# Attention scores by 64-key tiles in a fused attention and feed-forward kernel: eight tiles in the array, ten score steps per query block

## The chip, the cores and the metric

The kernel runs on one core of one Trainium2 chip. The metric is device time in microseconds (us), from the launch to the end on that core. A profile of one execution gives the span from the first to the last instruction, which is a little shorter than that time.

The core's engines appear under short names. PE is the matrix unit, TensorE; PEld is its loading of weights. DVE is VectorE, ACT is ScalarE, POOL is GpSimd, SP is the queue that issues most transfers. Matrix results land in PSUM, a small memory of eight banks that TensorE writes and VectorE and ScalarE read. Everything else lies in SBUF.

## The reference, cut to what matters

One layer norm feeds two branches, and both are added to the input.

```python
S, D = 2048, 448
def _A_ref(x, wqkv, wo):
    H = 16; Dh = D // H; W = 256            # 16 heads of 28
    q, k, v = ...                           # of x @ wqkv
    scores = jnp.einsum("bhqd,bhkd->bhqk", q, k) * (Dh ** -0.5)
    idx = jnp.arange(S)
    mask = (idx[:, None] - idx[None, :] >= 0) & (idx[:, None] - idx[None, :] < W)
    scores = jnp.where(mask[None, None], scores, -1e9)
    p = _softmax(scores, axis=-1)
    o = jnp.einsum("bhqk,bhkd->bhqd", p, v)
    return o.transpose(...).reshape(B, S, D) @ wo
def _B_ref(x, w_gate, w_up, w_down):        # F = 1792
    return (_gelu(x @ w_gate) * (x @ w_up)) @ w_down
xn = _layernorm(x, axis=-1)
return x + _A_ref(xn, A_wqkv, A_wo) + _B_ref(xn, B_w_gate, B_w_up, B_w_down)
```

A query sees only itself and the 255 keys before it. So 128 keys are seen by at most 383 queries, and 64 keys by at most 319.

## The kernel before

The 2048 tokens are worked through in four blocks of 512 queries (`qb` 0 to 3). The 16 heads are four groups `g` of four heads; each head has 32 of the 128 partitions (28 and padding). A block has two stretches. In the attention stretch, scores, exponentials and values of the four groups are interleaved with dense matrix work from "feeds": the output and down projection of the block before (`po`), the projections of the next block (`pv`, `pq`, `pk`), and some up projections ahead of time (`ue`). In the gated stretch the rest of gate (`gt`) and up (`u`) follows.

One group takes three score steps, so a block takes twelve. Each step fills the same PSUM tile of four banks, 512 columns for each of the four heads, from two key tiles of 128 keys:

```python
def pieces(qb, n):             # (key tile, first query, queries, column), and which columns are masked
    k = 4 * qb
    if n == 0:
        return [(k + 3, 384, 128, 0), (k, 0, 384, 128)], [(0, 2, True), (384, 1, False)]
    if n == 1:                 # (cut: block 0)
        return [(k + 1, 128, 384, 0), (k - 2, 0, 128, 384)], [(0, 1, True), (256, 2, False)]
    return [(k - 1, 0, 256, 0), (k + 2, 256, 256, 256)], [(128, 1, False), (256, 1, True)]

# attention(), one step: scores, exponential, masks        (score tile "s": one buffer)
for kt, q0, nq, col in pc:
    for j in range(4):
        r = slice(32 * j, 32 * j + 32)
        nc.tensor.matmul(ss[:, j, col:col + nq], lhsT=kT[r, g, kt * P:(kt + 1) * P],
                         rhs=qT[r, g, qb * QB + q0:qb * QB + q0 + nq], start=True, stop=True,
                         tile_position=(32 * j, 0), skip_group_check=True)
p_sb = work.tile([P, 4, QB], bf16, name="p_sb", bufs=4)
nc.scalar.activation(out=p_sb[:, :, 0:ncol], in_=ss[:, :, 0:ncol], func=ACT.Exp, scale=SCALE)
for col, nb, diag in runs:     # ... 128 or 256 columns of each head, on all partitions
    nc.gpsimd.affine_select(out=reg, in_=reg, pattern=mid + [[1 if diag else -1, P]], ...)
```

Four matmuls, each on 32 rows of the array, share it. The values of a group come one group later, at step 4, 7 or 10, and for the last group in the gated stretch. Four matmuls on 32 columns each share the array, and all 128 keys of a tile are contracted at once:

```python
def pv(g, steps):
    tag = "o" if qb == 0 else "m" if g < 3 else down_tag[0]
    ov = psum.tile([P, QB], f32, name="ov", tag=tag, bufs=2 if tag == "m" else 1)
    # ... for each piece and j in 0..3
    nc.tensor.matmul(ov[32 * j:32 * j + 32, q0:q0 + nq], lhsT=v_sb[:, kt, h, :], rhs=p_sb[:, j, col:col + nq],
                     start=..., stop=..., tile_position=(0, 32 * j), skip_group_check=True)
    oc = work.tile([P, QB], f32, name="oc", bufs=2)
    nc.vector.tensor_copy(out=oc[:, :], in_=ov[:, :])
```

A column of ones in `v_sb` gives the sum of the weights as one more row of `ov`. `inverse()` brings it out by two 32x32 transposes and a reciprocal on VectorE (`l1`, `l_all`, `ri`, `rb`), and `scale_o()` multiplies, on GpSimd:

```python
nc.gpsimd.tensor_tensor(out=oN[:, g, :], in0=oc[:, :], in1=rb[...], op=ALU.mult)
```

In blocks 1 and 2 the feeds carry one pair of up projections, in block 3 five, in block 0 two; each goes from PSUM to SBUF by two casts (`hT<-ue`), and the gate's result is multiplied onto it later (`hT<-ge,hT`). The other pairs take the gate times `u` from PSUM (`hT<-ge,u`). The feeds of blocks 1 to 3 use the two PSUM banks tagged "m".

Of the kernel before, what the change touches and what calls it, by code (L numbers as in the profile page):

```python
# [68 lines left out]
def drain(feeds):  # L69

    while any(f.gens for f in feeds):
        min((f for f in feeds if f.gens), key=lambda f: (f.held, f.closed)).run()
# [3 lines left out]
def kernel(  # L76
# [63 lines left out]

    eps_t = const.tile([P, 1], f32, name="eps_t")
    nc.vector.memset(eps_t[:, :], 1e-5)
    warm = const.tile([P, 512], bf16, name="warm")
    nc.vector.memset(warm[:, :], 0.0)
    wqp = const.tile([P, 3, H, 32], bf16, name="wqp")
    wkp = const.tile([P, 3, H, 32], bf16, name="wkp")
    w3p = const.tile([P, H, 32], bf16, name="w3p")
    nc.vector.memset(wqp[:, :, :, Dh:32], 0.0)
    nc.vector.memset(wkp[:, :, :, Dh:32], 0.0)
    nc.vector.memset(w3p[:, :, Dh:32], 0.0)  # L150
    nc.vector.memset(wo[:, :, :], 0.0)
    nc.scalar.preload_act_table_set("natural_log_exp_and_others")

    xnT = const.tile([P, 4, S], bf16, name="xnT")
# [6 lines left out]
    def warmup(n):  # L161
        wps = phase[0].pool.tile([P, 4, QB], f32, name="wps", tag="s")
        for i in range(n):
            nc.tensor.matmul(wps[:, i % 4, :], lhsT=warm[:, 0:P], rhs=warm[:, :], start=True, stop=True)


    def stat(t):
# [126 lines left out]
    def new_hT(qb):  # L294
        hT = blk.tile([P, NF, QB], bf16, name="hT", tag="hT")
        hTs[qb] = hT
# [81 lines left out]
                dense(b, False)  # L378
                end(b)

    def pieces(qb, n):

        k = 4 * qb
        if n == 0:
            return [(k + 3, 384, 128, 0), (k, 0, 384, 128)], [(0, 2, True), (384, 1, False)]
        if n == 1:
            if qb == 0:
                return [(k + 1, 128, 384, 0)], [(0, 1, True), (256, 1, False)]
            return [(k + 1, 128, 384, 0), (k - 2, 0, 128, 384)], [(0, 1, True), (256, 2, False)]
        if qb == 0:  # L390
            return [(k + 2, 256, 256, 0)], [(0, 1, True)]
        return [(k - 1, 0, 256, 0), (k + 2, 256, 256, 256)], [(128, 1, False), (256, 1, True)]

    def attention(qb, feeds, aux, plan):
        oN = blk.tile([P, 4, QB], bf16, name="oN")
        oNs[qb] = oN
        pend, copied, later = [], [], []

        def inverse():
            while copied:  # L400
                g, oc = copied.pop(0)
                l1 = work.tile([P, 16, 32], f32, name="l1", bufs=1)
                nc.vector.transpose(out=l1[:, :, :].rearrange("p a b -> p (a b)"), in_=oc[:, :])
                nc.vector.tensor_copy(out=l_all[:, 4 * qb + g, :], in_=l1[:, :, Dh])
                ri = work.tile([P, 16], f32, name="ri")
                nc.vector.reciprocal(out=ri[:, :], in_=l_all[:, 4 * qb + g, :])
                rb = work.tile([P, 16, 32], f32, name="rb", bufs=2)
                nc.vector.transpose(out=rb[:, :, :], in_=ri[:, :].unsqueeze(2).to_broadcast([P, 16, 32]))  # L408
                later.append((g, oc, rb))

        def scale_o():
            while later:
                g, oc, rb = later.pop(0)
                nc.gpsimd.tensor_tensor(out=oN[:, g, :], in0=oc[:, :], in1=rb[:, :, :].rearrange("p a b -> p (a b)"), op=ALU.mult)  # L414

        def pv(g, steps):

            tag = "o" if qb == 0 else "m" if g < 3 else down_tag[0]
            ov = psum.tile([P, QB], f32, name="ov", tag=tag, bufs=2 if tag == "m" else 1)
            for n, pc, p_sb in steps:  # L420
                for i, (kt, q0, nq, col) in enumerate(pc):
                    for j in range(4):
                        h = 4 * g + j
                        nc.tensor.matmul(ov[32 * j:32 * j + 32, q0:q0 + nq], lhsT=v_sb[:, kt, h, :], rhs=p_sb[:, j, col:col + nq],  # L424
                                         start=(n == 0 and i == 0), stop=(n == 2 and i == len(pc) - 1), tile_position=(0, 32 * j),
                                         skip_group_check=True)
            oc = work.tile([P, QB], f32, name="oc", bufs=2)
            nc.vector.tensor_copy(out=oc[:, :], in_=ov[:, :])  # L428
            copied.append((g, oc))

        if qb:
            feeds[0].run()
        for g in range(4):
            while (qb, g) not in done:
                feeds[0].run()
            group = []
            for n in range(3):
                pc, runs = pieces(qb, n)
                ncol = sum(x[2] for x in pc)
                for fd in feeds:  # L440
                    if fd.held:
                        fd.run()
                inverse()
                if n == 1 and g:
                    pv(g - 1, pend.pop(0))
                ss = phase[0].pool.tile([P, 4, QB], f32, name="sc", tag="s")
                for kt, q0, nq, col in pc:
                    for j in range(4):
                        r = slice(32 * j, 32 * j + 32)
                        nc.tensor.matmul(ss[:, j, col:col + nq], lhsT=kT[r, g, kt * P:(kt + 1) * P],  # L450
                                         rhs=qT[r, g, qb * QB + q0:qb * QB + q0 + nq], start=True, stop=True,
                                         tile_position=(32 * j, 0), skip_group_check=True)
                p_sb = work.tile([P, 4, QB], bf16, name="p_sb", bufs=4)
                nc.scalar.activation(out=p_sb[:, :, 0:ncol], in_=ss[:, :, 0:ncol], func=ACT.Exp, scale=SCALE)  # L454
                for col, nb, diag in runs:
                    reg = p_sb[:, :, col:col + nb * P]
                    if nb > 1:
                        reg = reg.rearrange("p h (b q) -> p h b q", q=P)
                    mid = [[0, 4], [0, nb]] if nb > 1 else [[0, 4]]
                    nc.gpsimd.affine_select(out=reg, in_=reg, pattern=mid + [[1 if diag else -1, P]], compare_op=ALU.is_ge,  # L460
                                            fill=0.0, base=0 if diag else -1, channel_multiplier=-1 if diag else 1)
                group.append((n, pc, p_sb))
                scale_o()
                left = 12 - 3 * g - n
                if left == 1:
                    drain(feeds)
                elif not qb:
                    share(feeds + [Feed()], 1e12, 0)
                else:
                    to = plan.get(12 - left, 0)  # L470
                    i = 12 - left
                    whole = sum(f.left for f in feeds) + STEP * left + PV * sum(j > i for j in (4, 7, 10))
                    ahead = STEP + (PV if n == 0 and g else 0) + (360 if to > 1000 else 0)
                    late = 400 if i == 0 else 0
                    share(feeds, (whole - late) / (left + 0.2) + late - ahead - to, to)
                if aux:
                    aux.pop(0)()
            pend.append(group)

        def rest():  # L480
            pv(3, pend.pop(0))
        def after():
            inverse()
            scale_o()
        return rest, after


# [63 lines left out]
    for qb in range(NB):  # L551
# [4 lines left out]
        if qb == 0:  # L556
            new_hT(0)
            early = (2, 8)
            feeds = [Feed((v23, 360), (gen_qk(0, (1, 2, 3)), 3 * QK1), (gen_proj(1), PROJ), (gen_up(0, early), UP1 * len(early)))]
            feeds[0].held = True  # L560
        else:
            ring[0] = ("m",)
            tags = "dodo" if last_tag[0] == "o" else "odod"
            feeds = [Feed((gen_down(qb - 1, tags), DOWN))]
            if qb < 3:
                feeds.append(Feed((gen_proj(qb + 1), PROJ)))
                new_hT(qb)
                early = (2,)
                feeds[1].gens.append(gen_up(qb, early))
                feeds[1].left += UP1  # L570
                plan = {0: 1140, 2: 1140, 4: 1300, 5: 1300, 7: 1300, 8: 1300, 10: 1300}
            else:
                new_hT(3)
                early = (2, 4, 6, 8, 10)
                feeds.append(Feed((gen_up(3, early), UP1 * len(early))))
                plan = {1: 1300, 4: 1300, 5: 1300, 7: 1300, 10: 1300}
        if qb:
            score_pool(1)
        rest, after = attention(qb, feeds, aux, plan)
# [19 lines left out]


    g1 = work.tile([P, 512], f32, name="g1", tag="l1", bufs=1)
    g2 = work.tile([P, 512], f32, name="g2", tag="rb", bufs=2)
    okc = const.tile([P, 1], f32, name="okc")
    okb = const.tile([P, 1], bf16, name="okb")
    one = const.tile([P, 1], bf16, name="one")
# [131 lines left out]
```

## Time and profile before

| | |
|---|---|
| time, median of 3 | 233.24 us (232.87 to 233.63) |
| span of the profiled execution | 230.8 us |
| mean granted TensorE clock | 0.997 |
| exponential `p_sb<-sc`, four heads of 512 columns | 40 times, mean 1877 ns |
| selects `p_sb<-p_sb`, 128x512 | 64 times, mean 634 ns |
| selects `p_sb<-p_sb`, 128x1024 | 28 times, mean 1098 ns |
| `oc<-ov` on VectorE | 16 times, mean 690 ns |
| `oN<-oc,rb` on GpSimd | 16 times, mean 1358 ns |
| score matmuls, value matmuls | 352 each |

How to read it. An engine's busy time is the time in which it had an instruction under way. Matmuls are pipelined, and each has a latency that the next one does not wait for; so a matmul's duration is longer than its cost, and the cost of a burst is read from its start to the start of what follows. A form such as `32*128 32x384` is a matmul on 32 rows and 128 columns of the array, with a moving operand of 32 partitions and 384 columns. In an answer of the timeline the columns are start, duration, engine, line, operation, tiles, form and count; in square brackets stands the engine's idle time before it and what ended it.

### The profile page before, as it was taken

To read this page: it belongs to the slowest core of one execution; us is meant where nothing else is said; L and a number is where in the kernel's file an instruction comes from. 1 tells how busy PE (TensorE), PEld (TensorE's weight loads), DVE (VectorE), ACT (ScalarE), POOL (GpSimd) and SP (SyncE) were. 2 spreads that over 40 slices of the span, in tenths; PEclk is the share of its full clock that TensorE was granted. 3 is DMA by queue.
4 is the path that set the end of the run, shared out by engine and by line. 5 is a ranking of instruction groups with operands and counts; after the bars stand their busy time and mean duration, and the time that the engine had idled before them with its cause. 6 is when DMAs were issued, how large, how long until landed. Compare 5 with 4: busy or idle time off the path is not lost.

```text
span 230.8 us, 4154 instructions
## 1 busy us (share of the span) xinstructions
PE 221.0 (96%) x1686; PEld 94.0 (41%) x1686; DVE 136.8 (59%) x280; ACT 135.1 (59%) x115; POOL 93.9 (41%) x116
## 2 busy tenths in 40 slices
PE   7889999999999999999999999999999999999990
PEld 2433333344443444344444444344444344334470
DVE  6996877869536676655534686464432866486210
ACT  3678897425967766333767767233687777363000
POOL 5024767220257877020066776320055877320000
PEclk9999999999999999999999999999999999999998
DMA  6917999012100000012100000000000000000010
GB/s 219 315 27 82 330 328 306 13 23 50 23 20 3 21 23 17 5 23 45 24 23 0 22 1 20 23 0 0 3 0 20 23 0 23 20 0 0 26 54 19
DMA packets 15682, 12.52 MB, mean 54 GB/s; under 512 B 7400, under 2 KB 14632, under 8 KB 15656
## 3 DMA queue, kind: packets, MB, share of 16 engines
q1 hardware_dynamic: 15112, 11.38, 17.7%
q10 hardware_dynamic: 544, 0.80, 1.0%
q8 instruction: 15, 0.25, 0.5%
q14 instruction: 11, 0.09, 0.1%
HBM read 8.77 MB, written 1.84 MB: 46 GB/s over the span
## 4 chain that ended last, share of the span: by engine, by line
PE 84%; ACT 5%; DVE 4%; DMA 2%; issue 1%; SPq 0%; ACTq 0%
PE po L285 18%; PE gt L202 16%; PE u L202 11%; PE sc L450 6%; PE gt L207 5%; PE po L280 5%; PE ov L424 4%; ACT p_sb L454 4%; PE pq L202 4%; PE ue L202 4%; PE pk L202 4%; PE pv L202 3%; DMA wv<-in_A_wqkv_dram 2%; PE pq L207 2%; PE ue L207 1%; DVE st L169 1%
## 5 line engine op out<-in xcount | busy, mean ns | idle before, releaser
L460 POOL TENSOR_SCALAR_AFFINE_SELECT p_sb<-p_sb 128x512 bf16<-128x512 bf16 (+1 forms) x92 | 69.4, 775 | 87.8 <-ACT p_sb L454 87.5
L454 ACT ACTIVATE p_sb<-sc 128x2048 bf16<-128x2048 f32 (+2 forms) x48 | 85.0, 1771 | 23.8 <-PE sc L450 22.2
L360 ACT ACTIVATE ge<-gt 128x1024 bf16<-128x1024 f32 x28 | 28.7, 1023 | 43.5 <-PE u L207 18.6
L285 PE MATMUL po<-wd,hT 128*128 128x448 bf16 (+1 forms) x238 | 50.1, 342 | 0.0
L202 PE MATMUL gt<-xnT,wg 128*128 128x512 bf16 x168 | 40.5, 380 | 0.0
L364 DVE TENSOR_TENSOR hT<-ge,u 128x512 bf16<-128x512 bf16 x38 | 24.4, 682 | 16.8 <-ACT ge L360 16.7
L414 POOL TENSOR_TENSOR oN<-oc,rb 128x512 bf16<-128x512 f32 x16 | 21.7, 1358 | 23.2 <-DVE rb L408 23.2
L285 PEld LDWEIGHTS <-hT 128*128 128x128 bf16 x238 | 21.6, 98 | 20.0 <-issue 4.0
L202 PE MATMUL u<-xnT,wu 128*128 128x512 bf16 x114 | 27.7, 379 | 0.0
L202 PEld LDWEIGHTS <-wg 128*128 128x128 bf16 x168 | 15.1, 98 | 22.1 <-issue 6.0
L202 PEld LDWEIGHTS <-wu 128*128 128x128 bf16 x168 | 15.7, 98 | 19.4 <-issue 1.8
L428 DVE COPY oc<-ov 128x512 f32<-128x512 f32 x16 | 11.0, 690 | 20.6 <-PE ov L424 19.3
L319 DVE CAST hT<-ue 128x512 bf16<-128x512 f32 x18 | 11.6, 685 | 14.1 <-PE ue L207 14.1
L450 PE MATMUL sc<-qT,kT 32*128 32x128 bf16 (+2 forms) x352 | 18.5, 275 | 1.0 <-ACT p_sb L454 0.6
L290 DVE TENSOR_TENSOR res<-po,x_sb 128x448 bf16<-128x448 f32 (+1 forms) x17 | 10.0, 590 | 11.1 <-PE po L285 11.1
L280 PE MATMUL po<-wo,oN 128*128 128x448 bf16 (+1 forms) x68 | 16.1, 342 | 0.0
L202 PE MATMUL pq<-xnT,wqp 128*128 128x512 bf16 (+1 forms) x51 | 13.3, 368 | 0.3 <-DVE v_sb L233 0.3
L202 PE MATMUL ue<-xnT,wu 128*128 128x512 bf16 x54 | 13.2, 380 | 0.0
L202 PE MATMUL pk<-xnT,wkp 128*128 128x512 bf16 (+1 forms) x51 | 13.1, 366 | 0.0
L424 PE MATMUL ov<-p_sb,v_sb 128*32 128x128 bf16 (+2 forms) x352 | 12.8, 277 | 0.2 <-DVE hT L319 0.2
L207 PE MATMUL gt<-xnT,wgu 64*128 64x512 bf16 x47 | 12.9, 380 | 0.0
L233 DVE CAST v_sb<-pv 128x448 bf16<-128x448 f32 x12 | 7.1, 618 | 9.6 <-PE pv L207 9.6
(67 smaller groups left out, 203.0 us busy)
## 6 DMA issues: line engine op xcount, KB each, us to landing
out_dram<-res SPq DMA_DIRECT2D x15, 112.0 KB, 1.7
wd<-in_B_w_down_dram SPq DMA_DIRECT2D x1, 1568.0 KB, 12.8
wu<-in_B_w_up_dram SPq DMA_DIRECT2D x1, 1344.0 KB
wg<-in_B_w_gate_dram SPq DMA_DIRECT2D x1, 1344.0 KB, 10.6
x_sb<-in_A_x_dram SPq DMA_DIRECT2D x1, 896.0 KB, 6.2
wraw<-in_A_wqkv_dram ACTq DMA_DIRECT2D x1, 672.0 KB, 5.0
x_sb<-in_A_x_dram SPq DMA_DIRECT2D x1, 448.0 KB, 5.3
wo<-in_A_wo_dram SPq DMA_DIRECT2D x4, 98.0 KB
```

The costliest lines, as they stand in the source:

```text
L202: nc.tensor.matmul(ps, lhsT=lhs(c), rhs=rhs(c), start=start and c == 0, stop=stop and c == 2, skip_group_check=True)
L207: nc.tensor.matmul(ps, lhsT=lhs[p0:p0 + 64], rhs=rhs[p0:p0 + 64], start=start, stop=stop, tile_position=(p0, 0), skip_group_check=True)
L280: nc.tensor.matmul(po[:, 0:w], lhsT=oN[:, g, cs], rhs=wo[:, g, lo:up], start=(g == 0), stop=False, skip_group_check=True)
L285: nc.tensor.matmul(po[:, 0:w], lhsT=hT[:, f, cs], rhs=wd[:, f, lo:up], start=False, stop=(f == NF - 1), skip_group_check=True)
L319: nc.vector.tensor_copy(out=hTs[qb][:, f + i, :], in_=us[i][:, :])
L360: nc.scalar.activation(out=ge[:, :, :], in_=pr["gt"][:, :, :], func=ACT.Gelu_apprx_tanh)
L364: nc.vector.tensor_tensor(out=hT[:, f + i, :], in0=ge[:, i, :], in1=u[:, :], op=ALU.mult)
L414: nc.gpsimd.tensor_tensor(out=oN[:, g, :], in0=oc[:, :], in1=rb[:, :, :].rearrange("p a b -> p (a b)"), op=ALU.mult)
L424: nc.tensor.matmul(ov[32 * j:32 * j + 32, q0:q0 + nq], lhsT=v_sb[:, kt, h, :], rhs=p_sb[:, j, col:col + nq], start=(n == 0 and i == 0), st ...
L450: nc.tensor.matmul(ss[:, j, col:col + nq], lhsT=kT[r, g, kt * P:(kt + 1) * P], rhs=qT[r, g, qb * QB + q0:qb * QB + q0 + nq], start=True, s ...
L454: nc.scalar.activation(out=p_sb[:, :, 0:ncol], in_=ss[:, :, 0:ncol], func=ACT.Exp, scale=SCALE)
L460: nc.gpsimd.affine_select(out=reg, in_=reg, pattern=mid + [[1 if diag else -1, P]], compare_op=ALU.is_ge, fill=0.0, base=0 if diag else -1 ...
```

## The change

From block 1 on, the scores are cut by 64 keys. A tile of 64 keys takes half of the array's columns, and two such tiles share a step: one on partitions 0 to 63, one on 64 to 127, each with its own queries ("skewed"). With four heads by two tiles, eight matmuls share the array. Since 64 keys are seen by fewer queries than 128, a group needs 2.5 steps rather than three: two of its own, and one shared with the neighbouring group. A block has ten steps. It is meant to lower the number of exponentials and the columns that TensorE streams.

What goes with it:

- The values contract 64 keys at a time: a group's halves accumulate in two PSUM banks. ScalarE copies one to SBUF (`oh`), and VectorE adds the other (`oc`). Values come at steps 4, 6 and 9.
- The masks are selects of 64 columns on 64 partitions: six, eight or four per step.
- From block 1 on, `oN` is multiplied on VectorE.
- Blocks 1 and 2 have no early up projection in their attention; all of it is in the gated stretch.
- `p_sb` has five buffers rather than four, `oc` and `rb` one rather than two, and `oh` shares the buffer of `l1`.
- The warm-up at the start multiplies zeros out of `wo`, whose memset goes first, and the tile `warm` goes.
- The plan of how much of the feeds goes between the steps is new.

```diff
-    def pieces(qb, n):
+    def steps_of(qb):
         k = 4 * qb
+        # (cut: block 0, the three steps per group as before)
+        def first(g):
+            return ([(g, 0, k, 0, 320, 0), (g, 1, k, 64, 320, 0), (g, 0, k - 1, 0, 192, 320), (g, 1, k + 2, 320, 192, 320)], 512,
+                    [(0, (0,), 64, True), (1, (0, 320), 64, True), (0, (256, 448), 64, False), (1, (256,), 64, False)])
+        def second(g):
+            return ([(g, 0, k + 1, 128, 320, 0), (g, 1, k + 1, 192, 320, 0), (g, 0, k + 3, 384, 128, 320), (g, 1, k + 3, 448, 64, 320),
+                     (g, 1, k - 2, 0, 128, 384), (g, 0, k - 2, 0, 64, 448)], 512,
+                    [(i, (0, 320), 64, True) for i in range(2)] + [(i, (256, 448), 64, False) for i in range(2)])
+        for g in (0, 2):
+            yield first(g)
+            yield second(g)
+            yield ([(g + i, h, k + 2 - 3 * h, 256 - 256 * h, 256, 256 * i) for i in range(2) for h in range(2)], 512,
+                   [(0, (0, 256), 64, True), (1, (192, 448), 64, False)])
+            yield first(g + 1)
+            yield second(g + 1)
 ...
-                rb = work.tile([P, 16, 32], f32, name="rb", bufs=2)
+                rb = work.tile([P, 16, 32], f32, name="rb", bufs=1)
-                nc.gpsimd.tensor_tensor(out=oN[:, g, :], in0=oc[:, :], ...)
+                (nc.vector if qb else nc.gpsimd).tensor_tensor(out=oN[:, g, :], in0=oc[:, :], ...)
 ...
+            tags = ("o",) if not qb else ("m", "m" if g < 3 else down_tag[0])
+            ov = [psum.tile([P, QB], f32, name="ov", tag=tag, bufs=2 if tag == "m" else 1) for tag in tags]
+                    nc.tensor.matmul(ov[half or 0][32 * j:32 * j + 32, q0:q0 + nq], lhsT=v_sb[r, kt, 4 * g + j, :],
+                                     rhs=p_sb[r, j, col:col + nq], start=..., stop=..., tile_position=(k0, 32 * j), ...)
+                nc.scalar.copy(out=oh[:, :], in_=ov[0][:, :])
+                nc.vector.tensor_tensor(out=oc[:, :], in0=oh[:, :], in1=ov[1][:, :], op=ALU.add)
 ...
+        pvs = {4: 0, 6: 1, 9: 2} if qb else {4: 0, 7: 1, 10: 2}
+                    nc.tensor.matmul(ss[k0:k0 + nk, j, col:col + nq], lhsT=kT[r, g, kt * P + k0:kt * P + k0 + nk],
+                                     rhs=qT[r, g, qb * QB + q0:qb * QB + q0 + nq], start=True, stop=True,
+                                     tile_position=(32 * j, k0), skip_group_check=True)
 ...
         def rest():
-            pv(3, pend.pop(0))
+            after()
+            pv(3)
 ...
-                new_hT(qb)
-                early = (2,)
-                feeds[1].gens.append(gen_up(qb, early))
-                feeds[1].left += UP1
-                plan = {0: 1140, 2: 1140, 4: 1300, 5: 1300, 7: 1300, 8: 1300, 10: 1300}
+                plan = {0: 1140, 1: 1140, 2: 1300, 4: 1300, 6: 1300, 7: 1300}
```

In a piece, the entries are group, half (0 or 1), key tile, first query, queries and first column; in a mask, half, columns, width and kind.

## The prediction

> **What bounds the kernel now.** I read the page first: TensorE is busy for nearly the whole span.
>
> ```profile
> PE 221.0 (96%) x1686; PEld 94.0 (41%) x1686; DVE 136.8 (59%) x280; ACT 135.1 (59%) x115; POOL 93.9 (41%) x116
> PE 84%; ACT 5%; DVE 4%; DMA 2%; issue 1%; SPq 0%; ACTq 0%
> ```
>
> The second line is the chain that ended last: 84% TensorE. Averages hide stages, so next the busy time in stretches. From the timeline I took the borders: the first `po` of a block, its first gate or up matmul (`u`), and the next block's first `po`. Blocks 1, 2 and 3 thus give an attention and a gated stretch each.
>
> ```profile
> 57.82:90.31 32.49, 32.46 (x298) 13.73 (x297) 19.30 (x36) 24.72 (x16) 20.19 (x25) 1.00 0.06 16
> 90.31:111.57 21.26, 21.26 (x130) 8.67 (x129) 12.26 (x26) 7.88 (x9) 3.56 (x4) 1.00 0.11 25
> 165.31:195.90 30.59, 29.87 (x282) 12.76 (x281) 16.31 (x30) 24.00 (x14) 19.81 (x25) 1.00 0.04 13
> 195.90:212.00 16.10, 16.10 (x102) 6.43 (x101) 9.62 (x16) 8.25 (x8) 3.94 (x4) 1.00 0.02 7
> ```
>
> Columns: stretch, length, then busy PE, weight load, VectorE, ScalarE, GpSimd. Blocks 1 and 2 never leave TensorE idle; only block 3 does (0.7 us), and there ScalarE is the pacemaker at times. The TensorE timeline of block 1 gives the price of the parts that change: read start to start, because the durations include the pipeline.
>
> ```profile
> 82.14 0.40 PE L450 MATMUL sc<-qT,kT 32*128 32x128 bf16 x8
> 82.47 1.31 PE L285 MATMUL po<-wd,hT 128*128 128x448 bf16 x6
> 83.61 0.54 PE L280 MATMUL po<-wo,oN 128*128 128x448 bf16 x2
> 84.08 0.84 PE L424 MATMUL ov<-p_sb,v_sb 128*32 128x128 bf16 x24
> 84.86 0.40 PE L450 MATMUL sc<-qT,kT 32*128 32x384 bf16 x8
> 85.19 1.47 PE L202 MATMUL ue<-xnT,wu 128*128 128x512 bf16 x6
> 86.49 0.54 PE L280 MATMUL po<-wo,oN 128*128 128x448 bf16 x2
> ```
>
> A burst of scores (512 columns for each of four row tiles) occupies 0.33 us, a burst of values (1536 columns for each of four column tiles) 0.78 us. Dense work (`ue`) costs 1.30/6 = 0.217 us per 512 columns: of a score burst 0.22 us is streaming and 0.11 the change of tiling and the issue; of the value burst 0.65 and 0.13. A dense run before a burst pays as well: the two `po` at 83.61 take 0.47, where two of 448 columns stream in 2 x 0.19. So each change of tiling is about 0.10 us.
>
> In block 3 ScalarE's timeline shows the other limit:
>
> ```profile
> 188.37 0.40 PE L450 MATMUL sc<-qT,kT 32*128 32x128 bf16 x8
> 190.82 0.40 PE L450 MATMUL sc<-qT,kT 32*128 32x384 bf16 x8
> 193.28 0.40 PE L450 MATMUL sc<-qT,kT 32*128 32x256 bf16 x8 [0.33 <-ACT p_sb L454]
> 188.90 1.88 ACT L454 ACTIVATE p_sb<-sc 128x2048 bf16<-128x2048 f32 x1 [0.58 <-PE sc L450]
> 191.35 1.88 ACT L454 ACTIVATE p_sb<-sc 128x2048 bf16<-128x2048 f32 x1 [0.58 <-PE sc L450]
> ```
>
> There is one score buffer, so scores and exponential alternate: 0.53 us from scores to exponential, 1.88 in it, 2.46 per step. Twelve such steps are 29.5 us of the stretch's 30.6, and the wait in the bracket is TensorE held up by it.
>
> **What the Trainium skill says.** "TensorE: Matmul & The Clock Gate", Part 3 (packing small matmuls), says that row and column tiles compose and matmuls on separate tiles run concurrently; it gives 10.6 times for sixteen tiles. The trace agrees for four tiles (0.21 us of streaming, not four times that); nothing in it shows eight. "TensorEngine Tiling (Array Packing)", Key Properties, says that changing the tiling mode drains the array: the 0.10 us above. "SBUF — State Buffer", Who interferes with whom, says that a VectorE instruction with two SBUF inputs and a GpSimd instruction that reads SBUF exclude each other. The trace agrees: the main VectorE form of this kind, `hT<-ge,hT`, has minimum, median and maximum
>
> ```profile
> L362 DVE TENSOR_TENSOR hT<-ge,hT x9: 649/659/1639, 45.9 to 209.2; 128x1024 bf16<-128x1024 bf16 x9
> ```
>
> and the 1639 lies under a GpSimd multiply `oN` of 1.62 us (the median of those is 1.27).
>
> **The change, part by part** (blocks 1 to 3; block 0 keeps its steps).
>
> Scores: ten bursts, not twelve. Each still streams 512 columns per tile, but as 16 or 24 matmuls over eight tiles. I allow 0.03 us more for the longer issue, and 0.05 more in the four bursts with six pieces, whose 64-column pieces stream only 0.027 us and may expose weight loads of about 0.09. Before: 12 x 0.33 = 3.96 us; after: 10 x 0.36 + 4 x 0.05 = 3.80. Two bursts less also save two exits, 0.20. Saved: 0.36 per block.
>
> Values: per group 1280 columns per tile, not 1536: 0.54 + 0.13 + about 0.06 for 48 matmuls in place of 24 = 0.73, against 0.78. Four groups: 0.20 per block.
>
> Early up projection: blocks 1 and 2 no longer do one pair of `ue` in attention but in the gated stretch. That moves about 1.5 us of TensorE work and removes one excursion into the half-row tiling (its halves now ride with the gate's): 0.2 to 0.3 saved. The instruction order shows 29 tiling changes where there were 34 in the attention of blocks 1 and 2, and 28 for 32 in block 3; this agrees with the two score bursts and the excursion.
>
> TensorE alone: 0.36 + 0.20 + 0.25 = 0.8 us in blocks 1 and 2 each, and 0.56 in block 3: 2.2 us.
>
> ScalarE: two exponentials less (3.76 us per block), four copies `oh` more (0.58 each, the ScalarE row of `qT<-pq` at the same size): 1.4 less. In blocks 1 and 2 this is beside TensorE and worth nothing. In block 3 ten steps of 2.46 are 24.6 us, under the TensorE work, so the waits on the exponential go. How much they are: 72 `po` x 0.19 + 5 `ue` pairs x 1.52 (with halves) + 12 x 0.33 + 3 x 0.78 + 17 further changes of tiling x 0.10 = 29.3, and the stretch has 30.6. The same sum for block 1 (with 1 `ue`, and 8.8 of projections for 4 of the `ue`) gives 32.2 of 32.5. So 1.3 - 0.3 = 1.0 us.
>
> Gross gain: 3.2 us.
>
> GpSimd: before, one group needs two selects of 128x1024 (1098 ns) and four of 128x512 (634 ns); after, a block has 64 selects on 64 partitions of 256 elements each. A line through the two sizes gives 170 + 0.906 x 256 = 402 ns; two in a row, of 634 and 1099, take 1.69 us in the timeline, so they overlap by 0.04: 0.36 us each, assuming half the partitions save nothing. A first step then has six (2.2 us), a second eight (2.9), a shared step four (1.4): 23.1 us per block in place of 18.6, less the multiplies (4 x 1.27) moved to VectorE. The load is bearable in 28 to 30 us of attention. The trouble is latency: the values of group 1 come at step 6, one step after the second step of that group (step 4). Adding block 3's bursts in the new order: 0.5 ahead, steps 0 to 3 of 3.2, 2.7, 2.8 and 1.95, values 0.7, so step 4 begins at 11.9; its exponential, delayed by `oh`, ends at 14.5, its eight selects at 17.5. Steps 4 and 5 take 2.8 and 1.95, so group 1's values start at 16.65 and reach that piece at 17.0. A wait of 0.5 us in each of three blocks: 1.5 us back. Groups 0 and 2 come out just without a wait, group 3 too (2.6 us of gate work stand ahead of it).
>
> VectorE: four `oN` multiplies of 128x512 fp32 with two SBUF inputs. I estimate 0.65 us from the 0.69 of `oc<-ov`. Three casts or products go in blocks 1 and 2. VectorE has room (19.3 of 32.5), but these multiplies exclude GpSimd and queue ahead of `oc = oh + ov`, which frees the bank that the next `pk` or `ue` needs. I count 0.15 us per block, 0.4 in all.
>
> Start: the warm-up now waits for the memset of `wo` (805 ns) rather than that of `warm` (272 ns). The first `pv` waits for the weights' transfer, which the chain shows ending at 7.41, so nothing.
>
> Sum: -3.2 + 1.5 + 0.4 = -1.3 us, and I lean to more, since a wait of half a microsecond needs several estimates to hold while the saved bursts do not. Prediction 231.0 us against 233.24, that is -2.2 us or 1.0%.
>
> **Rivals.** (1) Eight tiles pack badly: halves of the columns follow each other. Then scores cost 0.21 more in each of ten steps and values 0.53 more in each of four groups, 4.2 us per block, about 12 in all: 243. Against it, four tiles start within hundredths of a microsecond in every burst. I give 6%. (2) GpSimd becomes the bound: if a select on 64 partitions costs 450 ns per start, a second step takes 3.6 us, longer than most steps; values then wait 1 to 2 us in two groups of each block: 234 to 237. For it: 28.8 us of selects in a 28 to 30 us stretch. (3) The port: if back-to-back selects shut a VectorE multiply out until they pause, `oc` comes 2 us late and TensorE waits for a bank behind it: +1 to 1.5 per block, 233 to 235. (4) The better side: selects on the lower and upper 64 partitions run in part at once. "GPSIMD Engine Reference", 2.1 Instruction dispatch, says that a core starts the next instruction as soon as its own share is done; the 41 ns overlap fits that. Then no value waits, and 228.5 to 229.5 results.
>
> **Range and chances.** The sum lies near -2; the best case, everything overlapped, is about -5 (228.3). Waits of rivals 2 and 3 return up to 4. So 228.4 to 234.5. Two per cent faster would need less than 228.6: 0.12. Two per cent slower (over 237.9) needs rival 1 or rivals 2 and 3 together: 0.08.
>
> **What would show it.** Right: score bursts 0.35 to 0.40 us start to start, value bursts 0.70 to 0.75, 30 such score bursts in blocks 1 to 3; attention stretches about 30 us in blocks 1 and 2 (the moved pair lengthens the gated one by some 1.4) and 28.5 to 29 in block 3; the only new wait `ov` on GpSimd's `p_sb`, half a microsecond once a block. Wrong: score bursts of 0.5 us and more (rival 1); GpSimd over 95% busy in attention with `ov` waiting in several groups (rival 2); `oN` multiplies on VectorE of 1 us and more and `pk` or `ue` waiting for `oc` (rival 3).

## The result and the profile after

The changed kernel takes 231.86 us (median of 4 runs, 231.65 to 232.42), the kernel before 233.38 in 4 runs beside it: a ratio of 0.9941, with an interval of 0.9915 to 0.9967. The prediction was 231.0. The two large terms behind it were both too small, and they nearly cancel.

First the page of the changed kernel: the busy time of the engines.

```profile
PE 218.4 (95%) x2237; PEld 97.7 (43%) x2262; DVE 143.3 (62%) x289; ACT 129.4 (56%) x121; POOL 101.0 (44%) x224
```

TensorE is shown 2.6 us less busy (part of that is 25 missing matmul records: 2262 weight loads, 2237 matmuls), and the span is only 0.9 shorter (229.9 for 230.8). Next the stretches of the changed kernel: attention and gated of block 1, then of block 3, each from the first `po`, gate or up matmul to the next border. The columns are stretch, length, then busy PE, weight load, VectorE, ScalarE, GpSimd.

```profile
58.19:88.76 30.57, 30.28 (x454) 14.15 (x456) 17.85 (x32) 22.75 (x17) 23.75 (x58) 1.00 0.06 17
88.76:111.44 22.68, 22.31 (x159) 9.47 (x161) 15.84 (x32) 8.07 (x10) 2.37 (x6) 1.00 0.12 24
164.68:194.69 30.01, 28.99 (x445) 13.53 (x448) 16.63 (x28) 22.03 (x15) 23.41 (x58) 1.00 0.05 14
194.69:210.75 16.06, 15.19 (x118) 6.14 (x120) 10.83 (x20) 8.33 (x9) 2.70 (x7) 1.00 0.03 9
```

Block 1 as a whole went from 53.75 us to 53.25. Block 3's attention stretch went from 30.59 to 30.01 only, and TensorE is shown busy for 28.99 of it; 0.6 us of the rest is a wait that comes below, and where matmul records are missing the trace shows idle time too. (The prediction's last row for the kernel before runs to 212.00, past the first `po` of the end at 211.11, so the last gated stretch of the kernel before is 15.21 us.) Now TensorE's timeline of block 1, around the values of group 1; for every line the cost is the distance to the start of the next.

```profile
74.61 0.54 PE L279 MATMUL po<-wo,oN 128*128 128x448 bf16 x2
75.08 1.32 PE L453 MATMUL ov<-p_sb,v_sb 64*32 64x256 bf16 x48
76.33 0.43 PE L484 MATMUL sc<-qT,kT 32*64 32x320 bf16 x24
76.69 0.55 PE L279 MATMUL po<-wo,oN 128*128 128x448 bf16 x2
77.08 0.54 PE L284 MATMUL po<-wd,hT 128*128 128x448 bf16 x2
77.46 0.81 PE L201 MATMUL pq<-xnT,wqp 128*128 128x512 bf16 x2
78.31 0.81 PE L201 MATMUL pk<-xnT,wkp 128*128 128x512 bf16 x3
```

The scores take 0.36 us (76.33 to 76.69), with 24 small matmuls and even six pieces; bursts of 16 take 0.36 as well. The values of group 1 take 1.25 (75.08 to 76.33); group 0's take 0.68. Inside the burst the starts pause from 75.43 to 75.79 and from 75.95 to 76.17. The last two selects of step 4 begin at 75.325 and 75.698 and take 414 and 417 ns, so they end at 75.74 and 76.12:

```profile
75.33 0.41 POOL L419 TENSOR_SCALAR_AFFINE_SELECT p_sb<-p_sb 64x256 bf16<-64x256 bf16 x1
75.70 0.42 POOL L419 TENSOR_SCALAR_AFFINE_SELECT p_sb<-p_sb 64x256 bf16<-64x256 bf16 x1
75.79 0.32 PE L453 MATMUL ov<-p_sb,v_sb 64*32 64x320 bf16 x8
```

That is the wait of the prediction, 0.57 us long. No bracket marks it: the trace counts a stalled burst as busy, and the Trainium skill, "Perfetto Trace Analysis", Tensor Engine Instruction, says that a matmul's end in the trace is estimated and not observed. Only the distance of starts shows it. Behind it `pq` takes 0.84 (77.46 to 78.31) where three such matmuls take 0.65. VectorE's timeline of the changed kernel shows why:

```profile
74.42 0.70 DVE L431 STREAM_TRANSPOSE l<-oc 128x512 f32<-128x512 f32 x1
75.16 0.18 DVE L432 COPY l_all<-l 128x16 f32<-128x16 f32 x1
75.36 0.25 DVE L434 RECIPROCAL ri<-l_all 128x16 f32<-128x16 f32 x1
75.65 0.71 DVE L436 STREAM_TRANSPOSE rb<-ri 128x512 f32<-128x512 f32 x1
76.40 0.73 DVE L442 TENSOR_TENSOR oN<-oc,rb 128x512 bf16<-128x512 f32 x1
77.05 0.61 DVE L289 TENSOR_TENSOR res<-po,x_sb 128x448 bf16<-128x448 f32 x1
77.58 0.67 DVE L460 TENSOR_TENSOR oc<-oh,ov 128x512 f32<-128x512 f32 x1
```

`oc = oh + ov` gives the bank back that `pk` needs, and it ends at 78.25. It stands behind group 0's inverse and multiply. The same section of the skill says that VectorE works strictly in order; the trace agrees: ScalarE's copy `oh` ends at 77.11, and `oc` starts at 77.58, behind `res`.

In block 3 the same queue costs more. TensorE and VectorE of the changed kernel, at the values of group 2:

```profile
189.17 0.92 PE L279 MATMUL po<-wo,oN 128*128 128x448 bf16 x4
190.42 0.32 PE L453 MATMUL ov<-p_sb,v_sb 64*32 64x320 bf16 x4 [0.33 <-DVE hT L318]
191.01 0.73 PE L453 MATMUL ov<-p_sb,v_sb 64*32 64x320 bf16 x44 [0.28 <-DVE hT L318]
191.67 0.43 PE L484 MATMUL sc<-qT,kT 32*64 32x320 bf16 x24
...
189.01 0.75 DVE L442 TENSOR_TENSOR oN<-oc,rb 128x512 bf16<-128x512 f32 x1
189.68 1.27 DVE L318 CAST hT<-ue 128x512 bf16<-128x512 f32 x2
```

The values need the two banks of the last `ue` pair. The pair's last matmuls end at 188.12, and its casts started at 189.68, after group 1's inverse and its multiply. The four `po` take 1.25 instead of 0.77 and the burst 1.25 instead of 0.68: 1.05 us lost.

In block 3's gated stretch, group 3's inverse and multiply stand ahead of two products. ScalarE's `ge` waits for the products, and the next gate matmuls for `ge` (TensorE, ScalarE, then VectorE of the changed kernel):

```profile
206.01 1.46 PE L201 MATMUL gt<-xnT,wg 128*128 128x512 bf16 x6 [0.60 <-ACT ge L359]
204.93 1.94 ACT L359 ACTIVATE ge<-gt 128x1024 bf16<-128x1024 f32 x2 [1.65 <-DVE hT L361]
...
202.80 0.71 DVE L436 STREAM_TRANSPOSE rb<-ri 128x512 f32<-128x512 f32 x1
203.55 0.69 DVE L442 TENSOR_TENSOR oN<-oc,rb 128x512 bf16<-128x512 f32 x1
204.16 1.28 DVE L361 TENSOR_TENSOR hT<-ge,hT 128x1024 bf16<-128x1024 bf16 x2
```

Twelve gate matmuls take 3.45 us there, from 203.94, and the twelve before them 2.70: 0.75 lost.

### The profile page after: what moved, and what is told of

It is laid out like the page before. It is cut to its first block, busy times and chain, and to the rows that moved or that the text cites. A ratio compares the mean times of both kernels' runs of the same rounds, so it can differ in the third digit from the quotient of the medians.

```text
span 229.9 us, 5401 instructions
## 1 busy us (share of the span) xinstructions
PE 218.4 (95%) x2237; PEld 97.7 (43%) x2262; DVE 143.3 (62%) x289; ACT 129.4 (56%) x121; POOL 101.0 (44%) x224
## 5 line engine op out<-in xcount | busy, mean ns | idle before, releaser
L419 POOL TENSOR_SCALAR_AFFINE_SELECT p_sb<-p_sb 64x256 bf16<-64x256 bf16 (+2 forms) x212 | 92.6, 454 | 90.0 <-ACT p_sb L488 85.4
L488 ACT ACTIVATE p_sb<-sc 128x2048 bf16<-128x2048 f32 (+2 forms) x42 | 73.8, 1757 | 18.4 <-PE sc L484 18.4
L363 DVE TENSOR_TENSOR hT<-ge,u 128x512 bf16<-128x512 bf16 x42 | 26.8, 682 | 15.9 <-ACT ge L359 15.9
L201 PE MATMUL u<-xnT,wu 128*128 128x512 bf16 x120 | 30.2, 379 | 0.3
L484 PE MATMUL sc<-qT,kT 32*64 32x320 bf16 (+7 forms) x640 | 16.9, 263 | 0.4 <-ACT p_sb L488 0.3
L459 ACT COPY oh<-ov 128x512 f32<-128x512 f32 x12 | 7.0, 586 | 17.5 <-PE ov L453 17.5
L460 DVE TENSOR_TENSOR oc<-oh,ov 128x512 f32<-128x512 f32 x12 | 8.2, 685 | 12.5 <-ACT oh L459 12.4
L318 DVE CAST hT<-ue 128x512 bf16<-128x512 f32 x14 | 9.0, 685 | 9.0 <-PE ue L206 9.0
L453 PE MATMUL ov<-p_sb,v_sb 64*32 64x320 bf16 (+7 forms) x640 | 13.5, 258 | 0.9 <-DVE hT L318 0.6
L250 DVE CAST kT<-pk 128x512 bf16<-128x512 f32 (+1 forms) x17 | 10.9, 643 | 2.4 <-PE pk L206 2.4
```

Of the source, the lines that this page charges most:

```text
L201: nc.tensor.matmul(ps, lhsT=lhs(c), rhs=rhs(c), start=start and c == 0, stop=stop and c == 2, skip_group_check=True)
L250: nc.vector.tensor_copy(out=kT[:, g, ts], in_=pk[:, 0:n])
L363: nc.vector.tensor_tensor(out=hT[:, f + i, :], in0=ge[:, i, :], in1=u[:, :], op=ALU.mult)
L453: nc.tensor.matmul(ov[half or 0][32 * j:32 * j + 32, q0:q0 + nq], lhsT=v_sb[r, kt, 4 * g + j, :], rhs=p_sb[r, j, col:col + nq], start=n == ...
L484: nc.tensor.matmul(ss[k0:k0 + nk, j, col:col + nq], lhsT=kT[r, g, kt * P + k0:kt * P + k0 + nk], rhs=qT[r, g, qb * QB + q0:qb * QB + q0 + ...
```

## The experiments

All are the changed kernel with the edit shown. Stretches are read from the starts as above; "att" is attention, "gat" gated, with the block. Lengths in us:

| | gat 0 | att 1, att 2 each | gat 1, gat 2 each | att 3 | gat 3 |
|---|---|---|---|---|---|
| before | 19.59 | 32.48 | 21.26 | 30.59 | 15.21 |
| changed | 19.89 | 30.57 | 22.68 | 30.01 | 16.06 |
| e1_no_selects | 19.87 | 30.51 | 22.68 | 29.54 | 16.06 |
| e2_multiply_gpsimd | 19.88 | 34.64, 33.07 | 22.68 | 33.30 | 15.39 |
| e3_values_later | 19.88 | 30.11 | 22.68 | 28.98 | 16.06 |
| e6_last_on_gpsimd | 19.88 | 30.54 | 22.68 | 29.99 | 15.38 |
| e8_two_buffers | 19.59 | 30.35 | 22.68 | 29.05 | 16.06 |
| e9_no_selects_two_buffers | 19.59 | 29.77 | 22.68 | 28.46 | 16.06 |
| e10_later_deferred | 19.88 | 29.77 | 22.68 | 28.83 | 16.25 |
| e11_early_pair | 19.88 | 33.25 | 21.34 | 29.99 | 16.06 |
| e12_best | 19.59 | 29.77 | 22.68 | 28.83 | 15.58 |
| e13_deferred_only | 19.87 | 30.66 | 22.68 | 29.18 | 16.06 |

**The selects.** The masks are left out in blocks 1 to 3; all else stays.

```diff
-            for m in masks:
+            for m in masks if not qb else ():
```

> The changed kernel without any mask select in blocks 1 to 3 (the output lacks the masks there; matmuls, exponentials and all else stay). Theory A (the gain was given back to waits of the values for GpSimd's selects): the value bursts that took 1.25 us (group 1 of each block) and 0.90 us (group 3) fall to 0.68 to 0.71, so 0.57 + 0.22 us per block go, 2.4 in all: about 229.4 us. Theory B (VectorE's multiplies and chains hold the banks): group 2's burst in block 3 still waits about 0.6 of its 1.05 us and the gated stretch of block 3 keeps its stall of 0.75; if B is the larger part, the time stays above 230.8. Rival C (the streaming itself gained nothing): all value bursts as before, 231.9.

Measured: 231.76 us, ratio 0.9923 (0.9895 to 0.9951), against 0.9941 with the selects. Group 1's burst falls from 1.25 to 0.67, but in blocks 1 and 2 the stretch only by 0.06, because a second wait was hidden behind it (block 3's falls by 0.47). VectorE, then TensorE of this kernel, in block 1:

```profile
75.81 0.71 DVE L436 STREAM_TRANSPOSE rb<-ri 128x512 f32<-128x512 f32 x1
76.56 0.69 DVE L442 TENSOR_TENSOR oN<-oc,rb 128x512 bf16<-128x512 f32 x1
77.17 0.61 DVE L289 TENSOR_TENSOR res<-po,x_sb 128x448 bf16<-128x448 f32 x1
77.70 0.68 DVE L460 TENSOR_TENSOR oc<-oh,ov 128x512 f32<-128x512 f32 x1
...
77.04 0.81 PE L201 MATMUL pq<-xnT,wqp 128*128 128x512 bf16 x2
78.43 0.81 PE L201 MATMUL pk<-xnT,wkp 128*128 128x512 bf16 x3 [0.58 <-DVE oc L460]
```

The values finish 0.6 us earlier, the sum `oc` comes when VectorE's queue allows, and `pk` waits for it. So selects and VectorE's queue hold up the same work one after the other, and taking the first away only uncovers the second.

**The multiply back on GpSimd.**

```diff
-                (nc.vector if qb else nc.gpsimd).tensor_tensor(out=oN[:, g, :], in0=oc[:, :], ...)
+                nc.gpsimd.tensor_tensor(out=oN[:, g, :], in0=oc[:, :], ...)
```

> The changed kernel with only the multiply oN put back on GpSimd in blocks 1 to 3. Theory B (the multiply on VectorE delays the casts that free the m banks, and the gate products): block 3's group 2 no longer waits for the casts (1.0 us back) and its gated stall of 0.75 goes, so about 230.3. Theory A (GpSimd is the tight engine): two multiplies of 1.27 us each fall among the selects, the values of groups 2 and 3 wait 0.5 to 1 us more in every block, so 232 to 234. Both together: about 231.5, and the trace tells which stretches won and lost.

Measured: 240.85 us, ratio 1.0298 (1.0237 to 1.0358). The waits of VectorE, then of TensorE (total, times, longest):

```profile
DVE oc L460 <- POOL oN L442: 10.2, 3, 3.7
...
PE pk L201 <- DVE oc L460: 5.1, 2, 2.6
PE ue L201 <- DVE oc L460: 2.6, 1, 2.6
```

The GpSimd multiply stands behind the selects; with one `oc` buffer, `oc = oh + ov` waits until it has read the old sum. (TensorE's granted clock is 0.985 on the mean here, for 0.998; after the gap in block 1 six matmuls from 83.01 to 85.57 take 0.43 us each, twice the usual, and that is part of the loss.) So with one buffer of `oc` the multiply can't go back to this place in GpSimd's order; on GpSimd with two buffers, as in the kernel before, it was not run. The last gated stretch is back at 15.39. Group 2's burst in block 3 takes 0.68, but TensorE had waited for `oc` there before, so this run alone doesn't show what held it; the runs with another order on VectorE, further down, do.

**Group 3's multiply alone on GpSimd.**

```diff
-                (nc.vector if qb else nc.gpsimd).tensor_tensor(...)
+                (nc.vector if qb and g < 3 else nc.gpsimd).tensor_tensor(...)
```

> The changed kernel with the multiply oN of group 3 alone back on GpSimd, which is idle in the gated stretch. Theory B: VectorE's chain before the gate products of block 3 is 0.7 us shorter, and that stretch loses its stall of 0.75: 231.2 us. Rival: the products hT<-ge,hT have two SBUF inputs and are shut out while GpSimd multiplies (one took 1639 ns in the kernel before), so the stall stays within 0.2 us: 231.8.

Measured: 231.35 us, ratio 0.9907 (0.9876 to 0.9938). The last gated stretch falls from 16.06 to 15.38 and nothing else moves: 0.68 us belong to that one multiply ahead of the products. What the rival expected is seen but costs nothing: one product takes 1757 ns (650 to 694 in the changed kernel) under the GpSimd multiply, and TensorE doesn't wait for it.

**The values of group 1 a step later.**

```diff
-        pvs = {4: 0, 6: 1, 9: 2} if qb else {4: 0, 7: 1, 10: 2}
+        pvs = {4: 0, 7: 1, 9: 2} if qb else {4: 0, 7: 1, 10: 2}
-                plan = {0: 1140, 1: 1140, 2: 1300, 4: 1300, 6: 1300, 7: 1300}
+                plan = {0: 1140, 1: 1140, 2: 1300, 4: 1300, 5: 1300, 7: 1300}
```

(And step 6 becomes step 5 in block 3's plan.)

> The changed kernel with group 1's values at step 7 rather than 6 in blocks 1 to 3 (and the feed plan shifted by one, 6 to 5), nothing left out. Theory A: group 1's burst falls from 1.25 to about 0.70 in each block (1.7 us in all), and in block 3 VectorE's chain of group 1 comes after the casts rather than before them, so group 2's 1.05 us goes too: 229.2 us. Rival D (the waits only move on, because GpSimd is behind anyway): group 2 or 3 waits instead, 231.3 or more.

Measured: 230.2 us, ratio 0.9844 (0.9787 to 0.9902). The burst takes 1.02: 0.34 us of wait remain. What they wait for is no longer the selects but the cast `kT` (it ends at 78.64, and the burst resumes at 78.69), which stands behind group 0's multiply. In block 3 the pair's casts now come ahead of group 1's inverse, and group 2's burst takes 0.68.

**Two buffers, multiply behind the sum.** Two buffers for `oc` and `rb`, four for `p_sb` (for room), and the multiply issued one step after its inverse, behind that step's `oc = oh + ov`. Then the same with the masks left out in blocks 1 to 3, so that neither wait is there.

```diff
-        def scale_o():
-            while later:
+        def scale_o(keep=0):
+            while len(later) > keep:
 ...
+            old = len(later)
             inverse()
             if i in pvs:
                 pv(pvs[i])
+            if qb:
+                scale_o(len(later) - old)
 ...
-            scale_o()
+            if not qb:
+                scale_o()
```

> The changed kernel with two buffers for oc and rb (p_sb four for them), and the VectorE multiply oN of blocks 1 to 3 one step later, behind the sum oc of the next group or the casts; nothing left out. Theory E (two waits lie side by side: group 1's values wait for the selects, and behind them VectorE's chain holds the bank that the next pk or ue needs): in blocks 1 and 2 the selects still set the pace, group 1's burst stays at 1.25 us and the attention stretch gains 0.2 us at most; in block 3 the casts come 0.7 us sooner and group 2's burst loses half a microsecond or more; block 0's gated stretch loses its 0.29. About 231.0. Theory A alone (only selects matter): nothing beyond block 0's 0.3, 231.6.

> The same without the selects of blocks 1 to 3 (the output lacks the masks there). Without the selects alone the attention stretch of blocks 1 and 2 was 30.51 us against 30.57, though group 1's burst fell by 0.57: pk then waited for oc. Theory E: with VectorE's multiply out of oc's way that wait goes too, the stretch falls to 29.8 to 29.9, and block 3's to 28.6 to 28.9: about 229.5 us. If a third limit stands behind (ScalarE's exponentials, or the streaming itself), it stays at 30.3 or more.

Measured: 229.77 us, ratio 0.9843 (0.9787 to 0.9898), and without masks 228.66, ratio 0.9805 (0.9748 to 0.9862). Block 0's gated stretch is back at 19.59: there `oc`'s copy had waited 1.4 us for GpSimd's multiply. With masks, group 1's burst keeps its 0.57 and `pq` takes 0.65. Without them TensorE has no gap in the attention stretches (block 1, then block 3):

```profile
57.68:87.45 29.77, 29.77 (x457) 13.99 (x456) 17.58 (x32) 22.72 (x17) 0.00 (x0) 1.00 0.06 18
162.58:191.04 28.46, 28.46 (x449) 13.32 (x448) 16.10 (x28) 22.01 (x15) 0.00 (x0) 1.00 0.05 14
```

These are the floors of the new cut, with this plan of the feeds. Masks off with VectorE's queue as it was gave 0.06 in block 1, masks off after it was mended 0.58: the one hides behind the other.

**Order or buffer?** In both of these the multiply goes to the start of the next step, with single buffers; in the first the values also come a step later, as in e3_values_later.

```diff
             inverse()
             if i in pvs:
                 pv(pvs[i])
+            if qb:
+                scale_o()
 ...
-            scale_o()
+            if not qb:
+                scale_o()
```

> Group 1's values at step 7 (as in the run before, 230.2 us) with the VectorE multiply of blocks 1 to 3 at the start of the next step, behind the casts rather than ahead of them; single buffers as in the changed kernel, nothing left out. Theory E: the 0.34 us that group 1's burst still waited, for the bank that the cast of pk frees, goes in all three blocks: 1.0 us, 229.2. If that wait was for selects, the burst stays at 1.02 and the time at 230.2.

> The changed kernel with one difference: the VectorE multiply oN is issued at the start of the next step, behind oc = oh + ov and the casts, with single oc and rb buffers and values at step 6 as changed. If the order in VectorE's queue was the second wait, this alone gives most of what two buffers with the deferred multiply gave: attention of block 1 about 30.3 us (30.57 as changed), block 3's 29.1 (30.01), group 1's burst still 1.25, 229.9 us. If the second buffer of oc and rb was what helped, the order alone does nothing or less than nothing: 231.5 us or more, with copies oc waiting for oN.

Measured: 229.56 us, ratio 0.9835 (0.9777 to 0.9894), and for the order alone 231.23, ratio 0.9929 (0.9913 to 0.9945). Neither theory holds for the order alone. In block 3 it gives 0.83 us: the casts no longer wait for the multiply. VectorE of the second kernel (order alone):

```profile
188.52 0.71 DVE L436 STREAM_TRANSPOSE rb<-ri 128x512 f32<-128x512 f32 x1
189.16 1.25 DVE L318 CAST hT<-ue 128x512 bf16<-128x512 f32 x2
190.33 0.89 DVE L442 TENSOR_TENSOR oN<-oc,rb 128x512 bf16<-128x512 f32 x1
```

In blocks 1 and 2 it gives nothing (30.66 for 30.57): with one `oc` the multiply must read group 0's sum before group 1's may be written (it starts at 76.89 in this kernel, the sum at 77.78). There a second buffer helps, or later values. With later values the stretch is at its floor of 29.77, masks and all.

**The early pair back.** One pair of `ue` in the attention of blocks 1 and 2, as before; the plan of the feeds stays the new one.

```diff
+                new_hT(qb)
+                early = (2,)
+                feeds[1].gens.append(gen_up(qb, early))
+                feeds[1].left += UP1
```

> The changed kernel with the early pair of up projections of blocks 1 and 2 back in their attention stretch (it falls into the last step). The prediction put 0.25 us per block on moving it. If so: attention longer by about 1.6 us and the gated stretch shorter by about 1.4, in all 0.2 to 0.3 per block, 232.4 us. Rival: the early pair is a filler that hides waits, and the gated stretch is quicker with it, then 231.5 or less.

Measured: 234.56 us, ratio 1.0053 (1.0036 to 1.007): 1.35 us more per block than the change. In attention the pair takes 1.39 + 0.32 us, and the gated stretch gets 1.34 shorter: 0.37 for the pair's own matmuls, for an estimate of 0.25. The rest are waits. TensorE of this kernel:

```profile
86.12 0.32 PE L453 MATMUL ov<-p_sb,v_sb 64*32 64x320 bf16 x4
86.72 0.73 PE L453 MATMUL ov<-p_sb,v_sb 64*32 64x320 bf16 x44 [0.28 <-DVE kT L250]
...
91.82 1.46 PE L201 MATMUL u<-xnT,wu 128*128 128x512 bf16 x6 [0.78 <-DVE hT L318]
```

The pair lands last in the stretch, and the first `u` waits for its casts to free the banks. The feed also shifts, so that group 2's values meet a `kT` cast. A plan made for the pair was not tried, so 1.35 is not the price of the pair as such.

**All of it together.** The kernel of e10_later_deferred, with group 3's multiply on GpSimd and group 2's of block 0 on VectorE:

```diff
-                (nc.vector if qb else nc.gpsimd).tensor_tensor(...)
+                (nc.vector if (g < 3 if qb else g == 2) else nc.gpsimd).tensor_tensor(...)
```

> The kernel with group 1's values at step 7 and the VectorE multiply behind the casts, and besides: group 3's multiply on GpSimd, and in block 0 group 2's multiply on VectorE. If the stall of the last gated stretch comes from the chain and multiply before the products hT, and the 0.29 us of block 0 from the single oc buffer held by GpSimd's multiply, the two add to what the values at step 7 and the deferred multiply gave: last gated stretch 15.4 in place of 16.25, block 0's gated stretch 19.6 in place of 19.88, attention of block 1 unchanged at 29.8; 228.5 us. If group 3's GpSimd multiply now holds the single oc buffer or falls on the selects of the last step, the values of group 3 or the next block's first copy wait and it stays at 229.5 or above.

Measured: 228.71 us (227.8 to 229.0), ratio 0.981 (0.9791 to 0.983). It beats both kernels. Its four stretches, with all selects on GpSimd:

```profile
58.23:88.00 29.77, 29.77 (x457) 13.99 (x456) 17.81 (x32) 22.73 (x17) 23.67 (x58) 1.00 0.06 18
88.00:110.68 22.68, 22.68 (x162) 9.49 (x161) 15.36 (x31) 8.08 (x10) 3.74 (x8) 1.00 0.12 24
163.12:191.95 28.83, 28.83 (x450) 13.38 (x449) 16.09 (x28) 22.15 (x15) 22.96 (x56) 1.00 0.05 14
191.95:207.52 15.57, 15.53 (x121) 6.25 (x120) 11.30 (x19) 8.42 (x9) 5.25 (x10) 1.00 0.03 9
```

In block 1's attention GpSimd is as busy as in the changed kernel (23.67 for 23.75 us), and TensorE no longer waits. So there GpSimd's load wasn't the limit, only when its results were wanted. In block 3 two short waits for selects are left. Group 2's values take 0.84 us: their last pieces start at 188.71, after a select that ends at 188.66. Group 3's take 0.91, in the gated stretch (15.58 us, where 15.4 was expected), behind a select that takes 852 ns under group 2's multiply (VectorE, GpSimd, TensorE):

```profile
194.85 0.73 DVE L442 TENSOR_TENSOR oN<-oc,rb 128x512 bf16<-128x512 f32 x1
195.00 0.85 POOL L419 TENSOR_SCALAR_AFFINE_SELECT p_sb<-p_sb 64x256 bf16<-64x256 bf16 x1
195.91 0.24 PE L453 MATMUL ov<-p_sb,v_sb 64*32 64x128 bf16 x8
```

**The kernel before, again.** The stretches of the two traces differ by 0.4 us in sum, the times by 1.5. Nothing is edited here.

> The kernel before, unchanged, profiled a second time. The times say that the change is worth 1.5 us; the two traces' attention and gated stretches give 0.4 of it. In the first profile of the kernel before, the timed execution is 2.7 us longer than its span (233.5 against 230.8), and in those of the changed kernel and all its variants 1.7 to 1.9. If that microsecond belongs to the kernel before, this profile shows 2.5 us or more between time and span again. If it is chance of one execution, it shows 1.7 to 1.9, and its stretches are longer than in the first profile or its time about 232.5.

Measured: 233.12 us, ratio 1.0005 (0.9984 to 1.0025). All stretches repeat to 0.01 us. The profiled execution took 232.78 us with a span of 230.5: 2.3 us more than its span, between the two theories. The spans of all executions decide it. In 79 of the kernel before, the time is 2.13 to 3.03 us longer than the span (median 2.46); in 76 of the changed kernel and its variants it is 1.68 to 1.93 longer (median 1.77), once 2.26. So some 0.7 us of the gain lies outside the recorded span (0.6 to 0.9 by the medians of each run), where no view shows it; what it is stays open. The spans of the first two traces differ by 0.9, of which 0.4 is in the stretches and 0.5 at the end, where the last output takes 3.22 us from issue to landing before and 2.67 after. In the second trace of the kernel before it takes 2.79, and in all traces 2.67 to 3.33, so that half microsecond is not shown to come from the change.

## Why the prediction was right and where it failed

The stretches give the ledger. Gross gain from the floors: 2 x (32.48 - 29.77) - 2 x (22.68 - 21.26) in blocks 1 and 2, and (30.59 - 28.46) - (15.38 - 15.21) in block 3: 2.58 + 1.96 = 4.5 us. Returned: 2 x (30.57 - 29.77) + (30.01 - 28.46) + (16.06 - 15.38) + (19.89 - 19.59) = 4.1. The net is 0.4 of the measured 1.5; the rest lies outside the stretches, some 0.7 of it outside the span.

- **Gross gain, predicted 3.2, measured 4.5.** The mechanism was right, two sizes were too careful. Value bursts take 0.68 us, not 0.73, and those before took 0.87 once a block beside 0.77. The six-piece bursts cost 0.36 like the others; the 0.05 for exposed weight loads isn't there. That is about 0.2 us a block each, and the 0.8 per block became 1.29. Rival 1 is out: eight tiles pack as four did.
- **Group 1's values waiting for the selects, predicted 0.5 a block, measured 0.57.** Right in place; that the size fits so well is in part luck. A select starts every 0.415 us, not 0.36, so the last one of step 4 ends 17.93 us into the stretch and not at 17.5, but the values start later too (16.89 for 16.65). Selects on different halves don't overlap (below), so rival 4 is out. Rival 2 feared 0.45 us and two groups waiting; at 0.415 us only one group waits.
- **"Groups 0 and 2 come out just without a wait, group 3 too": failed for group 2 in block 3.** The wait of 1.05 us (1.25 twice, for 0.77 and 0.68) isn't for selects but for VectorE. The step looked only at GpSimd.
- **"I count 0.15 us per block, 0.4 in all" for VectorE: the term that failed.** The multiply itself costs 0.71 us, near the 0.65 estimated. But its place in VectorE's order, with the single buffers, costs 0.22 in blocks 1 and 2 each (30.35 with two buffers for 30.57), 1.0 in block 3's attention (29.05 for 30.01; 0.83 of it by the order alone), 0.68 in its gated stretch, and the single `oc` buffer 0.3 in block 0: 2.4 us. The first of these is the wait that the prediction had named (`oc` late for `pk`), at one and a half times the size; the others were missed. Its sign for block 3's attention, 28.5 to 29 us, was missed too (30.01), and came with the mended order (28.83).
- **Block 3's waits for the exponential, 1.0 predicted.** They were not measured apart. Of block 3's gross gain of 1.96, the scores and values would give about 0.9 (the 1.29 of blocks 1 and 2 less the 0.37 of the pair), which leaves 1.0. That agrees with the prediction but isn't shown.
- **Port lock (rival 3).** Seen, but small. The Trainium skill, "SBUF — State Buffer", Who interferes with whom, says that only one side holds the port. The trace of the changed kernel agrees: six of its 192 selects of this size take 766 to 846 ns, begun under a VectorE multiply, beside the usual 414, and `oN` itself takes hardly longer than the 0.69 us of the run without selects:

```profile
L442 DVE TENSOR_TENSOR oN<-oc,rb x12: 691/710/756, 76.4 to 203.5; 128x512 bf16<-128x512 f32 x12
L432 DVE COPY l_all<-l x16: 174/176/404, 26.2 to 202.3; 128x16 f32<-128x16 f32 x16
```

(minimum, median, maximum). VectorE wasn't shut out for microseconds; it came late by its own order. Here it is GpSimd that is held up, and in the kernel with all the changes together that costs TensorE the 0.2 us shown above.
- **The warm-up, nothing predicted.** It starts at 1.96 instead of 1.29 us, and the first `pv` at 7.51 instead of 7.46: hidden.

The sum of the steps was -1.3 us, and the stretches gave -0.4: 1.3 us too little gain had met 2.2 us too little loss. The lean to -2.2 came true for the gain and not for the loss. That the measured time, -1.5, lies near the forecast is partly luck: two errors cancel, and the larger part of it lies outside the stretches, which no step foresaw.

## What to carry to other kernels

When work moves to another engine, ask not only how long it takes there but what stands behind it in that engine's queue and who waits for that: a multiply of 0.71 us on an engine 60% busy cost up to 1 us at one place, together with its single buffers. A late result can be held by two waits in a row, as in block 1, so taking one away and seeing little change doesn't show that it was harmless; take both away to see the floor, and then find an order that reaches it. Read a matmul burst from start to start, as a stall inside it can count as busy.

## What was not expected of the hardware

- The score burst of 512 columns takes 0.36 us with 16 matmuls of 320 and 192 columns and with 24 of 64 to 320; two more sets of small pieces cost nothing.
- A select of 256 elements on 64 partitions takes 407 to 421 ns on either half when nothing holds it up. Within a step the next one starts 372 to 375 ns later when it is on the same half, and 456 to 468 ns later when it is on the other half: selects on one half overlap by some 40 ns, selects on different halves not at all.
- A tiny copy, `l_all<-l` (16 elements a partition), took 404 ns once beside its usual 174 while selects ran. In the two runs without selects in blocks 1 to 3 none takes more than 178 ns, so selects have to do with it; why most copies beside selects aren't slowed was not tried.
